# An accumulating DMA from GpSimd for the last step of most integer exponential chains, with products ordered by readiness and one set of planner limits

## The chip, the cores and the metric

The kernel runs on one core of a Trainium2 chip. The metric is the device time of one execution in microseconds. Five engines work side by side, each through its own instructions in a fixed order: PE (TensorE, matrix products), ACT (ScalarE, activations), DVE (VectorE), POOL (GpSimd) and SP (SyncE, which here issues DMAs). An engine that waits for a semaphore holds up everything that stands behind in its own order.

## The reference

The inputs are bf16. `x` has 2048 rows of 512. One branch is attention with 32 heads of 16, the other a mixer with shifted quarters of the columns and an MLP of width 1792; a sigmoid gate mixes the two. The reference, cut to what matters:

```python
def reference(A_x, A_wqkv, A_wo, B_x, B_w1, B_w2, B_w3, B_w4, gate_w):
    x = A_x                                           # 1 x 2048 x 512, bf16
    g = sigmoid((x * gate_w).sum(-1, keepdims=True))
    q, k, v = split_heads(x @ A_wqkv)                 # 32 heads of 16
    p = softmax(q @ k.T * 16 ** -0.5)                 # 2048 x 2048 per head
    a = merge_heads(p @ v) @ A_wo
    h = gelu(layernorm(x) @ B_w1)                     # 512 wide
    hs = shifted_quarters(h) @ B_w2                   # by +1, -1, +2, -2 rows
    x1 = x + hs
    b = x1 + gelu(layernorm(x1) @ B_w3) @ B_w4        # 512 -> 1792 -> 512
    return g * a + (1 - g) * b
```

## The kernel before

**Units, blocks and slots.** The attention is cut into 32 units: four chunks of 512 queries, and within each eight groups of four heads. A unit has 16 key tiles of 128 keys, and for each of them four heads, so 64 blocks of 128 keys by 512 queries. A score matmul (line 831) makes one block in PSUM. The blocks go round in slots: for each slot PE writes two or three blocks into the PSUM tile `stage`, and ACT turns them into exponentials in the SBUF ring `ring` with one activation of 1024 or 1536 columns (line 1228; in the first 34 slots into `pt`). There are two such tiles, so that PE may write the scores of slot k only when ACT is through with slot k-2. The products of the exponentials with the values (line 1241, `acc<-ring,vp`) follow in the PSUM tile `acc`. An extra column of ones in `vp` gives the denominators.

**Chains.** ACT does not take all blocks. In many slots with two blocks for ACT a third one, in the PSUM tile `dsc` beside them, goes to DVE. DVE adds a constant to the scaled score and writes an int16 (line 1048, the "dump"); these bits, read as bf16, are a piecewise linear exponential. Four blocks of one key tile are gathered in one tile of 128 x 4 x 512, 4 KB in each partition, and start a chain (the function `whole`): the exponential is smoothed by summing four copies of the bits that are shifted by `STEPS` (0, -31, -62, -95) and multiplied with weighted values (`vp` with weight 1 for the first two, `vw` with the other two weights). So a chain has three steps: each reads a term, adds an int16 constant to 128 x 2048 elements and writes another term. Steps run on DVE (line 1113) or on POOL (line 1111), whichever the planner offers them to. Each of the four terms is multiplied on PE with the values of the four heads, which makes 16 product matmuls a chain. The terms live in tiles of a pool called `room`: `quad` (three tiles), `more`, `xT` and `lent` are the names of the buffers that it is made of.

**What sets the order.** The order on every engine is planned while the program is written. A loop in Python keeps a planned time for each engine (`free`), asks for the possible next pieces of work of PE, ACT, DVE and POOL, and writes down the one that can start first. It uses fixed costs, and limits read by `rule(name)` for the unit in which the scores stand: a few usual ones (`USUAL`), and other values for many units (`RULES`). Among the limits are `CHAINS` (chains open at once), `NEED`, `AHEAD` and `HURRY` (how far ahead of a unit's end its chains start or press), `PTS` and `MANY` (how many exponentials or products may wait), `PMAX` (steps of a chain on POOL) and `BACK` (how far DVE has to be behind before POOL takes a step). The order that results is fixed in the program; the chip then runs it with semaphores. Where the plan sees PE idle for some tenths of a microsecond, the function `fill` puts a product with zeros (`acc<-wq,zero`).

`produce` puts a term's products in the list `products`, sorted by unit, in the order in which the terms are made; `attend` takes them from the front of that list. `step` makes a term from another one of the chain, `used` runs when a term's products have been placed and gives tiles back, and `opens` starts a chain after its last dump.

**Other work.** The projections, the mixer and the MLP fill PE between slots; their results leave PSUM through DVE. GELU runs on ACT between the exponentials, with a load of its table. At a unit's end DVE copies `acc` to `accsb`; SP sends the denominators through `den`, `rec_d` and the broadcast `bcs` (three DMAs, lines 1331 to 1340), and POOL multiplies (`oT<-accsb,bcs`, line 1353). POOL also does the layernorm's scaling (`xn`) and the second half of each `qT`. The limits for DVE and POOL know of a port that the two share: `post(..., shared=True)` keeps the planned time of a step on DVE away from that of one on POOL, and `behind` orders a POOL instruction after the last such step of DVE.

## Time and profile before

| what | value |
|---|---|
| median of 3 runs | 748.69 us (748.12 to 748.73) |
| the profiled execution | 748.4 us |
| its span, from the first to the last instruction | 746.6 us |
| granted TensorE clock | 1.000 |
| busy: PE, ACT, DVE, POOL | 730.8, 729.8, 683.6, 339.3 us |
| instructions: PE, ACT, DVE, POOL | 9866, 731, 1178, 295 |
| DMA: packets, bytes | 52306, 29.03 MB |

The profiled execution's own time is 1.8 us above its span, which is what lies around the first and the last instruction. "Busy" is the share of the span in which an instruction of the engine was under way; instructions overlap a little in the pipelines, and the ends of matmuls are modelled, so that a busy engine may still have small stalls inside. In a row of groups stand the line, the engine, the operation, the names written and read, their shapes and the number of instructions, then the group's busy time in us and the mean duration of one in ns, then the idle time of the engine just before them and who ended it.

### The profile page before, as it was taken

What the parts mean: (1) busy time and instruction counts of PE and PEld (TensorE: products, weight loads), DVE (VectorE), ACT (ScalarE), POOL (GpSimd) and SP (SyncE); (2) the same over time, 40 slices, a digit from 0 to 9 for tenths busy, and PEclk for the clock granted to TensorE, in tenths of its full rate; (3) what the DMA queues carried; (4) which work ended last, traced back from release to release, by engine and by line L of the source; (5) the groups of instructions that cost most, each with busy time, mean ns of one, the idle gap of its engine ahead of it and who ended that gap; (6) DMA issues with size and microseconds to landing.
All of it is one profiled execution on the core that took longest, in us unless ns stands there. A gap on an engine that the chain in (4) does not pass through costs nothing.

```text
span 746.6 us, 23400 instructions
## 1 busy us (share of the span) xinstructions
PE 730.8 (98%) x9866; PEld 230.9 (31%) x9866; DVE 683.6 (92%) x1178; ACT 729.8 (98%) x731; POOL 339.3 (45%) x295
## 2 busy tenths in 40 slices
PE   8999999999999999999999999999999999999997
PEld 4333332322332333332222332222322222322232
DVE  5799999999999998689999989999799999999994
ACT  6999999999999999999999999999999999999995
POOL 3734426444455456325564533454335455345420
PEclk9999999999999999999999999999999999999999
DMA  9400006201130060050001020000201000000011
GB/s 197 124 17 13 13 21 104 47 26 41 34 119 21 18 142 10 21 49 16 20 28 34 14 47 18 19 12 15 56 25 33 6 21 20 26 18 20 15 34 42
DMA packets 52306, 29.03 MB, mean 39 GB/s; under 512 B 36712, under 2 KB 47720, under 8 KB 52200
## 3 DMA queue, kind: packets, MB, share of 16 engines
q1 hardware_dynamic: 51240, 27.00, 15.1%
q8 instruction: 77, 1.26, 0.7%
q10 hardware_dynamic: 960, 0.52, 0.2%
q14 instruction: 29, 0.24, 0.1%
HBM read 17.17 MB, written 2.35 MB: 26 GB/s over the span
## 4 chain that ended last, share of the span: by engine, by line
PE 45%; ACT 41%; issue 10%; DVE 4%; DVEq 0%; ACTq 0%
ACT ring L1228 35%; PE acc L1241 16%; PE stage L831 14%; PE ps L301 6%; ACT pt L1228 3%; PE ps_o L301 2%; PE ps_y L301 2%; PE stage L301 1%; ACT g2T L1205 1%; DVE quad L1048 1%; ACT hT L1205 1%; ACT g2T L1208 1%; DVE xT L1048 1%; PE acc L301 1%; PE ps_q L301 1%
## 5 line engine op out<-in xcount | busy, mean ns | idle before, releaser
L1228 ACT ACTIVATE ring<-stage 128x1024 bf16<-128x1024 f32 (+1 forms) x649 | 648.3, 1159 | 1.9 <-PE dsc L831 0.5
L831 PE MATMUL stage<-qT,kT 32*128 32x512 bf16 (+2 forms) x1530 | 269.1, 380 | 6.0 <-ACT ring L1228 3.1
L831 PE MATMUL dsc<-qT,kT 16*128 16x512 bf16 (+1 forms) x542 | 208.2, 384 | 0.1
L831 PEld LDWEIGHTS <-kT 32*128 32x128 bf16 (+1 forms) x2072 | 77.0, 91 | 278.4 <-issue 250.9
L1048 DVE TENSOR_SCALAR quad<-dsc 128x512 int16<-128x512 f32 x235 | 155.1, 683 | 7.5 <-PE dsc L831 6.5
L1241 PE MATMUL acc<-ring,vp 128*17 128x512 bf16 (+3 forms) x1436 | 133.1, 378 | 1.3 <-DVE accsb L1402 0.5
L1111 POOL TENSOR_SCALAR quad<-quad 128x2048 int16<-128x2048 int16 x36 | 68.4, 1901 | 67.9 <-DVE quad L1113 22.9
L1048 DVE TENSOR_SCALAR more<-dsc 128x512 int16<-128x512 f32 x129 | 85.4, 683 | 5.5 <-PE dsc L831 4.5
L1048 DVE TENSOR_SCALAR xT<-dsc 128x512 int16<-128x512 f32 x122 | 80.5, 683 | 3.1 <-PE dsc L831 2.6
L1241 PEld LDWEIGHTS <-vp 128*17 128x17 bf16 (+1 forms) x2640 | 56.4, 89 | 81.4 <-issue 62.2
L301 PE MATMUL ps<-w,g2T 128*32 128x512 bf16 x896 | 70.2, 383 | 0.0
L1111 POOL TENSOR_SCALAR more<-more 128x2048 int16<-128x2048 int16 x20 | 38.0, 1900 | 56.8 <-DVE quad L1113 30.7
L1353 POOL TENSOR_TENSOR oT<-accsb,bcs 128x512 bf16<-128x512 f32 x29 | 37.1, 1279 | 44.6 <-DVE quad L1113 22.2
L301 PE MATMUL ps_y<-xnT,w 128*32 128x512 bf16 x704 | 54.8, 383 | 0.3 <-DVE qT L351 0.3
L1113 DVE TENSOR_SCALAR quad<-quad 128x2048 int16<-128x2048 int16 x61 | 45.6, 748 | 0.7 <-PE acc L1241 0.7
L1241 PE MATMUL acc<-quad,vp 128*17 128x512 bf16 x492 | 45.8, 381 | 0.0
L1111 POOL TENSOR_SCALAR xT<-xT 128x2048 int16<-128x2048 int16 x16 | 30.4, 1901 | 33.1 <-DVE xT L1113 7.0
L1241 PE MATMUL acc<-quad,vw 128*17 128x512 bf16 x468 | 45.2, 381 | 0.0
L1111 POOL TENSOR_SCALAR more<-quad 128x2048 int16<-128x2048 int16 x14 | 26.6, 1901 | 27.7 <-DVE quad L1113 8.1
L1048 DVE TENSOR_SCALAR lent<-dsc 128x512 int16<-128x512 f32 x56 | 37.2, 682 | 1.5 <-PE dsc L831 1.2
L1241 PEld LDWEIGHTS <-vw 128*17 128x17 bf16 x1136 | 27.8, 88 | 33.7 <-issue 25.7
L301 PEld LDWEIGHTS <-w 128*32 128x32 bf16 x1152 | 26.1, 95 | 35.3 <-issue 19.4
(146 smaller groups left out, 943.8 us busy)
## 6 DMA issues: line engine op xcount, KB each, us to landing
bcs<-rec_d SPq DMA_DIRECT2D x31, 256.0 KB
w<-in_B_w_dram SPq DMA_DIRECT2D x2, 1792.0 KB
x_sb<-in_A_x_dram SPq DMA_DIRECT2D x14, 128.0 KB
oT<-oT SPq DMA_DIRECT2D x112, 16.0 KB
out_dram<-ot SPq DMA_DIRECT2D x12, 128.0 KB
w<-in_B_w_dram SPq DMA_DIRECT2D x2, 512.0 KB
wkv<-in_A_wqkv_dram SPq DMA_DIRECT2D x1, 512.0 KB
wo_all<-in_A_wo_dram SPq DMA_DIRECT2D x8, 64.0 KB
```

What stands on the lines that cost most here:

```text
L301: nc.tensor.matmul(out[j:j + 32, :], lhsT=lhsT[:, j:j + 32], rhs=rhs, tile_position=(0, j), **kwargs)
L831: nc.tensor.matmul(out, lhsT=kT[G][32 * j:32 * j + K, cc, o:o + P], rhs=qTs[(c, G)][32 * j:32 * j + K, a, lo:hi], start=True, stop=True, t ...
L1048: nc.vector.tensor_scalar(out=bits[:, r:r + wide, :], in0=dsc.rearrange("p (a c) -> p a c", c=CH), scalar1=SHIFT, scalar2=LOWEST, op0=ALU. ...
L1111: behind(nc.gpsimd.tensor_scalar(out=to, in0=base["tile"], scalar1=1.0, scalar2=shift, op0=ALU.mult, op1=ALU.add))
L1113: fast["ins"] = nc.vector.tensor_scalar(out=to, in0=base["tile"], scalar1=shift, scalar2=None, op0=ALU.add)
L1205: nc.scalar.activation(out=part, in_=part, func=ACT.Gelu_apprx_tanh)
L1208: nc.scalar.activation(out=dst, in_=stages.pop(k)[:, 0:len(ms) * CH].rearrange("p (a c) -> p a c", c=CH), func=ACT.Gelu_apprx_tanh)
L1228: nc.scalar.activation(out=pt[:, 0:w], in_=stages.pop(k)[:, 0:w], func=ACT.Exp, scale=LN2 / 128.0)
L1241: nc.tensor.matmul(accs[n][32 * j:32 * j + M, lo:hi], lhsT=lhsT, rhs=p, start=(kt == 0), stop=(kt == NT - 1), skip_group_check=True, tile_ ...
L1353: behind(nc.gpsimd.tensor_tensor(out=oT, in0=tiles["accsb"][:], in1=tiles["bcs"][:], op=ALU.mult))
```

## The change

The last of the four terms (shift -95) is no longer made from another term by DVE or POOL in most chains. A tile of the constant -95 (`STEPS[-1] - STEPS[0]`, int16) is written once, at the start, to DRAM: POOL sets four columns of `ring`, and SP sends them to `down_d` behind the transposes of `xT`. Later, once the products of a chain's first term have been placed (`used`), POOL issues a DMA that adds `down_d` onto that first term's own tile, 128 x 2048 int16 (the function `flies`, with `accum_op=ALU.add`). Such a chain has two steps left on DVE or POOL, its steps take the newest term as their base, and its fourth term needs no further tile. A chain becomes one of this kind when fewer than `FLOWN` others (2, or 3 in units 1 to 31) have such a DMA planned or under way and it is not of the last unit. The planner's times for it are `FLIGHT`: 1.1 on POOL, 3.0 between two DMAs, 1.5 until the data have landed.

Two more things change. `produce` sorts the products of a unit by the planned time at which they are ready, where they stood in the order of their making. And `RULES` has one and the same set of limits for all units from 1 to 31, where many units had values of their own. The diff, with one line of each old and new table:

```diff
--- before.py
+++ after.py
@@ -115,6 +115,7 @@
     identf = const.tile([P, P], F32, name="identf")
     minus = const.tile([P, P], BF16, name="minus")
     rec_d = dpool.tile([NC_ * NU, 4, CH], F32, name="rec_d")
+    down_d = dpool.tile([P, 4, CH], I16, name="down_d")
 
     def wview(w):
         return w.rearrange("(kt p) c -> p kt c", p=P)
@@ -139,6 +140,9 @@
     nc.sync.dma_start(out=wkv[:, :, D:2 * D], in_=wview(A_wqkv[:, 2 * D:3 * D]))
     for c in range(1, NC_):
         nc.sync.dma_start(out=xT[c][:], in_=x_flat[c * CH:(c + 1) * CH, :], transpose=True)
+    down = ring[:, 4:8, :].bitcast(I16)
+    nc.gpsimd.memset(down, int(STEPS[-1] - STEPS[0]))
+    nc.sync.dma_start(out=down_d[:], in_=down)
     nc.gpsimd.memset(wo_pad[:], 0.0)
     nc.gpsimd.memset(pick[:], 0.0)
     for j in range(4):
@@ -167,31 +171,39 @@
 
 
 
-    USUAL = {'WIDE': 1, 'NEED': 14, 'AHEAD': 12, 'HURRY': 32, 'DLIM': 1.2, 'MANY': 8, 'PTS': 5, 'CHAINS': 2, 'MAXD': 28, 'PMAX': 3, 'BACK': 1.2, 'SHORT': 1}
+    USUAL = {'WIDE': 1, 'NEED': 14, 'AHEAD': 12, 'HURRY': 32, 'DLIM': 1.2, 'MANY': 8, 'PTS': 5, 'CHAINS': 2, 'MAXD': 28, 'PMAX': 3, 'BACK': 1.2, 'SHORT': 1, 'FLOWN': 2}
     RULES = {
-        2: {'NEED': 8, 'AHEAD': 8, 'HURRY': 14, 'DLIM': 0.9, 'MANY': 4, 'PTS': 7, 'CHAINS': 3, 'MAXD': 20, 'PMAX': 2, 'BACK': 0.9, 'SHORT': 3},
...
+        1: {'NEED': 20, 'AHEAD': 8, 'HURRY': 0, 'PTS': 6, 'PMAX': 1, 'BACK': 0.6, 'FLOWN': 3},
...
     }
     MM = 0.214
     TURN = 0.104
@@ -222,6 +234,7 @@
     DFILL = 1
     SLACK = 0.25
     GAP = 0.3
+    FLIGHT = (1.1, 3.0, 1.5)
     AGE = 4.0
     ARANK = 3
     LAG = 2.0
@@ -233,7 +246,7 @@
     free = {"pe": NOWFREE, "act": NOWFREE, "vector": NOWFREE, "pool": NOWFREE}
     queue = {"pe": [], "act": [], "vector": [], "pool": []}
     state = {"n": 0, "gen": 0, "young": True, "mm": 0, "sp": 0.0, "before": True, "after": False, "aside": 0.0, "kind": "", "t": 0.0, "piece": 0.0,
-             "credit": 0.0, "mixable": 0, "done": False, "ending": False, "acc": 0.0, "raw": 0, "moved": False, "accsb": 0.0, "slot": 0, "outs": 0, "bank": 0}
+             "credit": 0.0, "mixable": 0, "done": False, "ending": False, "acc": 0.0, "raw": 0, "moved": False, "accsb": 0.0, "slot": 0, "outs": 0, "bank": 0, "flown": 0.0}
     asides = deque()
     at = {}
     banks = {0: 0.0, 1: 0.0, 2: 0.0}
@@ -260,6 +273,7 @@
         return sum(min(b, t) - max(a, t - WINDOW) for a, b in busy if b > t - WINDOW) / WINDOW
 
     fast = {"ins": None}
+    flown = []
 
     def behind(ins):
 
@@ -1017,7 +1031,7 @@
 
     def produce(n, *term):
         i = len(products)
-        while i and products[i - 1][0] > n:
+        while i and (products[i - 1][0], products[i - 1][4]) > (n, term[3]):
             i -= 1
         products.insert(i, (n, *term))
 
@@ -1053,7 +1067,7 @@
             if full:
                 post("vector", rank(), 0.69, opens, begins(end), True)
 
-        terms, chain = [], {"next": 1, "pool": 0, "held": 2, "left": 0, "offers": []}
+        terms, chain = [], {"next": 1, "pool": 0, "held": 2, "left": 0, "offers": [], "flown": False}
 
         def give(tile, t):
             freed[id(tile)] = t
@@ -1066,6 +1080,8 @@
         def used(term):
             def go(t):
                 term["free"] = max(t, term["read"])
+                if chain["flown"] and not term["i"]:
+                    return post("pool", -1, FLIGHT[0], lambda end: flies(term["tile"], end), term["free"])
                 spare = [x for x in terms if x["free"] is not None and not x["gone"]]
                 if len(spare) > chain["left"]:
                     spare[0]["gone"] = True
@@ -1076,6 +1092,14 @@
             term = {"tile": tile, "i": i, "free": None, "gone": False, "read": 0.0}
             terms.append(term)
             produce(n, kt, heads, tile, end + HOLD[other], i == len(STEPS) - 1, used(term), i)
+
+        def flies(tile, end):
+            behind(nc.gpsimd.dma_start(out=tile, in_=down_d[:], accum_op=ALU.add))
+            state["flown"] = max(state["flown"], end) + FLIGHT[1]
+            lands = state["flown"] + FLIGHT[2]
+            flown.remove(None)
+            flown.append(lands)
+            produce(n, kt, heads, tile, lands, True, lambda t: give(tile, t), len(STEPS) - 1)
 
         def ready_tile(end):
             def go():
@@ -1091,7 +1115,7 @@
             i = chain["next"]
             chain["next"] += 1
             done = [x for x in terms if x["free"] is not None and not x["gone"] and x["free"] <= end - cost]
-            base = next(x for x in terms if not x["gone"])
+            base = terms[-1] if chain["flown"] else next(x for x in terms if not x["gone"])
             if chain["held"]:
                 chain["held"] -= 1
                 chain["times"].pop(0)
@@ -1119,7 +1143,7 @@
                         x["gone"] = True
                         give(x["tile"], x["free"])
             chain["pool"] += other
-            if chain["left"] == 1:
+            if chain["left"] == 1 - chain["flown"]:
                 quad["chains"] -= 1
 
         def opens(end):
@@ -1129,6 +1153,12 @@
             chain["tiles"] = [room.popleft(), room.popleft()]
             chain["times"] = [freed.get(id(x), 0.0) for x in chain["tiles"]]
             add(bits, 0, end - 0.69)
+            while flown and min(x or 1e9 for x in flown) < end:
+                flown.remove(min(x or 1e9 for x in flown))
+            if len(flown) < rule("FLOWN") and n < len(units) - 1:
+                chain["flown"] = terms[0]["gone"] = True
+                chain["left"] -= 1
+                flown.append(None)
             one(end, False, 0.69)
             offer("pool", 1.9, end)
 
```

The whole program is planned anew, so that nearly every row moves. Counted in the two orders: the steps of chains are 303 on DVE and 123 on POOL before, 242 and 50 in the change; POOL has 134 DMAs onto terms that were not there. The number of chains is 142 in both (2272 products of terms, 16 a chain). ACT has 535 activations of 1024 columns and 114 of 1536 into `ring` before, 532 and 116 in the change; together with the 34 into `pt` that is 1480 blocks in both. The products with zeros are 328 matmuls before and 408 in the change, four of which run side by side.

The first place is POOL in the middle of the program, where its steps stand between the multiplications `oT`. Before (`quad`, `more` and `xT` are tiles of `room`; behind each row the semaphores that it waits for, where PE, DVE or Pool is an engine and DMAHW a DMA issued by SP):

```order
L1353 TENSOR_TENSOR oT<-accsb,bcs 128x512 [waits DMAHW4_49,DMAHW3_49,DMAHW5_49,DMAHW2_49,DMAHW0_49]
L1353 TENSOR_TENSOR oT<-accsb,bcs 128x512 [waits DMAHW3_49,DMAHW2_49,DMAHW4_49,DMAHW1_49,DMAHW7_49,DVE_49,Pool_49]
L1111 TENSOR_SCALAR more<-more 128x2048 [waits DVE_49,PE_49] x2
L1111 TENSOR_SCALAR quad_273<-quad_273 128x2048 [waits DVE_49,PE_49]
L1111 TENSOR_SCALAR more<-quad_272 128x2048 [waits DVE_49,PE_49]
L1111 TENSOR_SCALAR xT_113<-quad_272 128x2048 [waits PE_49]
L1111 TENSOR_SCALAR more<-quad_274 128x2048 [waits DVE_49,PE_49]
L1111 TENSOR_SCALAR quad_273<-quad_273 128x2048 [waits DVE_49,PE_49]
L1111 TENSOR_SCALAR quad_273<-quad_272 128x2048 [waits DVE_49,PE_49,Pool_49]
L1353 TENSOR_TENSOR oT<-accsb,bcs 128x512 [waits DMAHW6_49,DMAHW5_49,DMAHW7_49,DMAHW4_49,DMAHW2_49]
```

In the change, at such a place (DMASW is a DMA issued by POOL):

```order
L1097 DMA xT_114<-down_d 128x2048 [waits DMASW0_49,DVE_49,PE_49]
L1135 TENSOR_SCALAR xT_113<-more 128x2048 [waits DVE_49,PE_49]
L1097 DMA quad_277<-down_d 128x2048 [waits PE_49]
L1097 DMA more<-down_d 128x2048 [waits DMASW6_49,DVE_49,PE_49]
L1097 DMA quad_275<-down_d 128x2048 [waits PE_49]
L1097 DMA quad_276<-down_d 128x2048 [waits DMASW4_49,DVE_49,PE_49]
L1135 TENSOR_SCALAR more<-xT_114 128x2048 [waits DMASW2_49,DVE_49,PE_49]
L1383 TENSOR_TENSOR oT<-accsb,bcs 128x512 [waits DMAHW5_49,DMAHW4_49,DMAHW6_49,DMAHW3_49,Pool_49]
L371 TENSOR_SCALAR qT<-qT,second 128x512 [waits DVE_49]
L1097 DMA more<-down_d 128x2048 [waits DMASW5_49,DVE_49,PE_49]
```

Between two `oT` there were seven steps in this piece; now there are DMAs and one step. Each DMA waits for PE, which has to be through with the first term's products, and everything behind it on POOL waits as well.

The second place is PE, where it reads a term that another engine has made. Before, for a term that POOL wrote (`stage` and `dsc` are the scores of one slot, `vw_162` the weighted values):

```order
L831 MATMUL stage<-qT,kT_141 128x512 [waits Activation_49]
L831 LDWEIGHTS kT_141
L831 MATMUL stage<-qT,kT_141 128x512
L831 LDWEIGHTS kT_141
L831 MATMUL dsc<-qT,kT_141 128x512 [waits DVE_49]
L1241 LDWEIGHTS vw_162
L1241 MATMUL acc<-more,vw_162 17x512 [waits Pool_49]
```

In the change, for the term that the row `DMA quad_277<-down_d` of the piece above makes. First the end of the products of that tile's first use, as first term, with the unweighted values `vp_157`; the DMA waits for these:

```order
L1271 MATMUL acc<-quad_277,vp_157 17x512
L1271 LDWEIGHTS vp_157
L1271 MATMUL acc<-quad_277,vp_157 17x512
L1271 LDWEIGHTS vp_157
L1271 MATMUL acc<-more,vp_157 17x512
L1271 LDWEIGHTS vp_157
```

Then, with the scores of six slots in between, the place where PE reads the same tile again as fourth term, with the weighted values `vw_163`:

```order
L845 MATMUL dsc<-qT,kT_138 128x512 [waits DVE_49]
L1271 LDWEIGHTS vw_161
L1271 MATMUL acc<-xT_113,vw_161 17x512
L1271 LDWEIGHTS vw_161
L1271 MATMUL acc<-xT_113,vw_161 17x512
L1271 LDWEIGHTS vw_161
L1271 MATMUL acc<-xT_113,vw_161 17x512
L1271 LDWEIGHTS vw_161
L1271 MATMUL acc<-xT_113,vw_161 17x512
L1271 LDWEIGHTS vw_163
L1271 MATMUL acc<-quad_277,vw_163 17x512 [waits DMASW1_49]
```

The wait for Pool has become a wait for a DMA that POOL issues, and the time that this DMA has is the time that PE takes from the one place to the other. Counted in the order in the same way, of the 133 DMAs that wait for PE 33 have six slots or fewer in between (nine of them five or fewer), 31 have seven, and 69 have eight to fourteen.

52 lines of the change are left out of this document (30 added, 22 removed).

## The prediction

> **What bounds the kernel now.** I read the page first: the span, the busy times and the chain that ended last.
>
> ```profile
> span 746.6 us, 23400 instructions
> PE 730.8 (98%) x9866; PEld 230.9 (31%) x9866; DVE 683.6 (92%) x1178; ACT 729.8 (98%) x731; POOL 339.3 (45%) x295
> PE 45%; ACT 41%; issue 10%; DVE 4%; DVEq 0%; ACTq 0%
> ```
>
> PE and ACT are both at 98% and share the chain between them; DVE, which the change relieves, has 4% of it. Next come the groups of ACT, first from the page, then by shape.
>
> ```profile
> L1228 ACT ACTIVATE ring<-stage 128x1024 bf16<-128x1024 f32 (+1 forms) x649 | 648.3, 1159 | 1.9 <-PE dsc L831 0.5
> ...
> L1228 ACT ACTIVATE ring<-stage 128x1024 bf16<-128x1024 f32 x535 | 505.0, 1082 | 1.5 <-PE dsc L831 0.5
> L1228 ACT ACTIVATE ring<-stage 128x1536 bf16<-128x1536 f32 x114 | 163.0, 1517 | 0.5 <-PE stage L831 0.3
> L1228 ACT ACTIVATE pt<-stage 128x1024 bf16<-128x1024 f32 x34 | 31.4, 1091 | 0.6 <-PE stage L831 0.5
> ```
>
> The exponentials take 648.3 + 31.4 = 679.7 us, with 2.6 us of visible idle time. Whether small waits are hidden inside, the timeline of ACT tells where it runs without any: the start of a tight run, and the start of one further on in the same run.
>
> ```profile
> 17.56 11.10 ACT L1228 ACTIVATE pt<-stage 128x1024 bf16<-128x1024 f32 x12
> 27.50 1.16 ACT L1228 ACTIVATE pt<-stage 128x1024 bf16<-128x1024 f32 x1
> 732.15 5.48 ACT L1228 ACTIVATE ring<-stage 128x1536 bf16<-128x1536 f32 x4
> 733.48 1.46 ACT L1228 ACTIVATE ring<-stage 128x1536 bf16<-128x1536 f32 x1
> ```
>
> Eleven activations of 1024 columns later is 9.94 us later, 0.904 us each; one of 1536 takes 1.33 us. So 569 x 0.904 + 114 x 1.33 = 666.0 us is what the exponentials cost when PE is always in time. They take 679.7 + 2.6 = 682.3, so about 16.3 us of the span are scores that come late. This is all that a better order can win as long as ACT keeps its blocks.
>
> Who makes the scores late? The waits of PE's weight loads and of PE (us in total, times, the longest):
>
> ```profile
> PEld L831 <- issue: 250.9, 648, 0.7
> ...
> PEld L831 <- DVE quad L1048: 7.3, 18, 0.6
> PEld L831 <- DVE xT L1048: 4.2, 10, 0.4
> PEld L831 <- DVE quad L1113: 3.8, 9, 0.4
> PEld L831 <- DVE more L1113: 3.0, 7, 0.4
> PEld L831 <- DVE more L1048: 2.1, 5, 0.4
> ...
> PEld L831 <- DVE lent L1048: 1.3, 3, 0.4
> ...
> PE stage L831 <- ACT ring L1228: 3.1, 11, 0.5
> ```
>
> A load for scores that waits for nobody has 250.9 / 648 = 0.39 us of idle time before it. The 52 that DVE released have 21.7 us, 0.42 each, so DVE added only 21.7 - 52 x 0.39 = 1.4 us. Most of the 16.3 us are not DVE's: PE is late because it is just at something else in its order.
>
> **The change part by part.** *ACT's work.* By the order there are 3 activations of 1024 fewer and 2 of 1536 more: -3 x 0.904 + 2 x 1.33 = -0.05 us, nothing. The number of chains is the same, 142, so no block leaves ACT.
>
> *Steps taken off DVE and POOL.* All steps of DVE, then all of POOL:
>
> ```profile
> 0.00:746.70 746.70, 207.89 (x303) 1.00 0.16 39
> ...
> 0.00:746.70 746.70, 233.74 (x123) 1.00 0.16 39
> ```
>
> A step is 207.89 / 303 = 0.686 us on DVE and 233.74 / 123 = 1.90 us on POOL. DVE loses 61 steps, 41.8 us, and falls to some 642 us; POOL loses 73, 138.7 us. None of this is on the path by itself. What it can win is lateness: at least 0, at most the 16.3 us. I take the 1.4 us that DVE visibly added, and of the other 14.9 us a share of 0.17, a little under the 61/303 = 0.20 by which DVE's steps become fewer, since the evictions that scores wait for most (line 1048) stay as they are: 1.4 + 2.6 = 4.0 us. Low and high end are 0 and -16.3.
>
> *134 issues on POOL.* No DMA is issued by POOL before. The nearest rows are SP's issue of a broadcast and POOL's own pass over such a tile (1.90 us):
>
> ```profile
> L1340 SPq DMA_DIRECT2D bcs<-rec_d x31: 562/577/594, 45.5 to 725.9; - x31
> ```
>
> Between 0.58 and 1.90 us I take 1.1, the planner's own figure in the diff: 134 x 1.1 = 147 us, so that POOL stays about as busy as it was (339.3 - 138.7 + 147 = 348 of 747). Covered: POOL is free half of the time. But POOL works in order, and a DMA that waits for PE's products holds up the next DMA, the steps, `xn` and `oT` behind it; `oT` in turn holds up DMAs while `bcs` has not landed.
>
> *The flight.* It has two bounds in the trace. A load of weights moves at 332 to 355 GB/s, and the 256 KB of one `bcs`, issued at 45.46, are through before 50.4:
>
> ```profile
> 211.60:213.60 2.00, 1.90 (x35) 0.81 (x29) 1.97 (x4) 2.00 (x3) 0.00 (x0) 1.00 1.03 332
> 264.20:266.20 2.00, 1.93 (x30) 0.70 (x26) 1.95 (x5) 2.00 (x3) 1.90 (x2) 1.00 1.03 355
> ...
> 45.46 0.58 SPq L1340 DMA_DIRECT2D bcs<-rec_d  x1
> ...
> 46.40:47.40 1.00, 1.00 (x26) 0.49 (x27) 1.00 (x2) 1.00 (x2) 0.82 (x2) 1.00 0.14 39
> 48.40:49.40 1.00, 1.00 (x23) 0.47 (x20) 1.00 (x3) 1.00 (x2) 0.00 (x0) 1.00 0.26 100
> 49.40:50.40 1.00, 1.00 (x19) 0.26 (x11) 1.00 (x3) 1.00 (x3) 0.00 (x0) 1.00 0.05 18
> 50.40:51.40 1.00, 1.00 (x17) 0.26 (x9) 1.00 (x4) 1.00 (x3) 0.00 (x0) 1.00 0.00 0
> ```
>
> A term has 524,288 bytes, 1.5 us at the pace of the load and 3.0 if adding in place moves them twice; at the pace of `bcs` (about 3 us for half as much) it is 6. Ahead of that stand some 1.4 us from the issue of `bcs` to its first bytes (45.46 to about 46.8, by the rise in the rows). So from PE's last product on the first term to the use of the fourth it is at least 1.5 + 1.4 = 2.9 us and at most 6 + 1.4 = 7.4. I take 6.0, because the plan spaces for 1.1 + 3.0 + 1.5 = 5.6, whose middle term is the doubled load, and 0.39 us is the nearest row for a hand-over to PE. By *DMA: Bandwidth & Descriptors*, section "Anatomy of one DMA — SWDGE (gpsimd) path", in the Trainium skill, such a DMA takes 2.0 us plus its bytes at 436 GB/s, here an estimate of 3.2 us, or 4.4 with the bytes twice; by that no term would be late and the sum would be that of the first rival, 744.4. No run here shows it.
>
> What is there for it: ACT's work on slots begins at 9.07 and its last four activations, in the row above, end at 732.15 + 5.48 = 737.63.
>
> ```profile
> 9.07 31.50 ACT L1228 ACTIVATE pt<-stage 128x1024 bf16<-128x1024 f32 x34 [0.50 <-PE stage L831]
> ```
>
> With 14 of GELU there are 697 slots in these 728.6 us, 1.05 us a slot. Six slots are 6.3 us, seven 7.3. By the order 33 of 133 flights have six slots or fewer, so a flight of 6.0 is just in time. What makes it late is company. The 31 `bcs` move 3 us each, and a flight moves 3.0; with 134 flights in 690 us, one in 5.15, each `bcs` meets (3 + 3) / 5.15 = 1.17 of them, 36 in all, and delays them by half its time, 1.5 us. A quarter of these (33/133), 9, are of the tight ones, late by 6.0 + 1.5 - 6.3 = 1.2 us. ACT has a cushion: while PE waits one activation still runs, 0.904 us, less the 0.384 of a score matmul:
>
> ```profile
> L831 PE MATMUL stage<-qT,kT x1530: 214/384/386, 8.6 to 735.3; 16*128 16x512 bf16 x94, 32*128 32x512 bf16 x93, 32*128 32x128 bf16 x3, 32*128 32x256 bf16 x2
> ```
>
> That is 0.52 us. So 9 x (1.2 - 0.52) = 6.1 us. With the short flight this term is 0, with the long one some 20 to 45.
>
> *The rest.* `bcs` itself may be delayed by a flight; before, the engines of its readers sat idle for it three times in all:
>
> ```profile
>   DMA bcs<-rec_d: 7.9, 3
> ```
>
> Nothing taken, up to 2 us if it reaches PE through `accsb`. The constant's write at the start stands on SP's queue ahead of twelve loads of `x_sb` and takes at most 1.5 us of the DMA engines; nothing taken. The 80 further zero matmuls are 20 groups of 0.22 us and stand where the plan sees PE idle: nothing taken, 4.4 at most. The new limits and the sorting of products change which piece of PE's work stands ahead of which slot; before, this made most of the 16.3 us, and I see no reason for a sign.
>
> The sum against the profiled execution: 748.4 - 4.0 + 6.1 = 750.5. The median of the runs is 0.3 above it, so 750.8.
>
> **The rivals.** *All terms in time.* If a flight is under 6.3 + 0.52 - 1.5 = 5.3 us, even a delayed one costs nothing, and 748.4 - 4.0 = 744.4 is left, 744.7 against the median. For it speaks the pace of the weight loads; against it that adding in place has to read what it writes.
>
> *Nothing reaches ACT.* DVE's relief was never on the path (1.4 us seen), and the terms are in time or the two cancel: 748 to 750. The change then doesn't do what it is named for.
>
> *Long flights.* From 6.8 us on, also flights without company are late. At 7.4, 33 x (7.4 - 6.3 - 0.52) = 19 us and more for those with company: 765 to 785. For it speaks the pace of `bcs`.
>
> *The port.* POOL's steps often begin when one of DVE has ended:
>
> ```profile
> L1111 POOL TENSOR_SCALAR quad<-quad 128x2048 int16<-128x2048 int16 x36 | 68.4, 1901 | 67.9 <-DVE quad L1113 22.9 <-DVE xT L1113 15.9 <-DVE more L1113 12.0
> ```
>
> The plan keeps the two apart. If a step of DVE that comes while POOL issues delays the DMA by its 0.69 us, the nine late ones lose 9 x 0.69 = 6.2 us more: 757. *SBUF — State Buffer*, "Who interferes with whom", in the Trainium skill says that a step of DVE that uses both its ports shuts GpSimd out while it writes the descriptors of a DMA; the trace agrees only in that the two alternate.
>
> **How the numbers follow.** A few terms late, 750.8: 0.34. All in time, 744.7: 0.32. Nothing reaches ACT, 749: 0.19. The port, 757: 0.06. Long flights, 765 and up: 0.09. The first, fourth and fifth are slower, 0.49 in all, the second is faster; the bound for a difference is 0.2%, 1.5 us, about what this kernel's measurement can tell. The forecast is that of the first. It stands only just above that bound, and its own range is 750.2 to 757, from one delayed term less than counted to twice as many. Over all, 743 leaves out 0.08 of the second case, where more than a third of the hidden lateness goes, and 764 the fifth.
>
> **What would show it.** In the profile after, ACT's exponentials and their idle time should again sum to some 682 us, DVE's steps to 166 us, POOL's to 95. PE's waits for DMAs issued by POOL should be some ten, of about a microsecond. If they are none, the flight is shorter than 5.3 us and the second rival holds; if over thirty, it is longer than 6.8. The forecast is wrong in its sign if the new order brings the scores in time for reasons of PE's own work, which I could not price.

## The result: 870.5 us, 16% slower, and the profile after

The median of four runs of the change is 870.54 us (865.02 to 883.16), that of the kernel before beside it 748.71. The ratio is 1.160, with a 95% interval of 1.154 to 1.167; the longest run, 883.16, is not in it. The forecast of 750.8 and the range up to 764 were wrong by far. The profiled execution took 873.04 us. A flight is, as in the prediction, one of the 134 DMAs that POOL issues onto a first term; a flown term is what it leaves in the tile. From the page:

```profile
span 871.2 us, 23744 instructions
...
PE 806.9 (93%) x9946; PEld 232.4 (27%) x9946; DVE 661.7 (76%) x1113; ACT 745.4 (86%) x730; POOL 327.4 (38%) x357
...
PEclk9996998867779898999999999879699888999779
DMA  9364549777946496566576775548755566667621
...
q0 software_dynamic: 19296, 70.26, 47.0%
q1 hardware_dynamic: 51384, 27.53, 15.0%
...
PE 52%; DMA 22%; ACT 9%; DVE 6%; issue 6%; SPq 4%; POOL 1%; DVEq 0%; POOLq 0%; ACTq 0%
...
L1258 ACT ACTIVATE ring<-stage 128x1024 bf16<-128x1024 f32 (+1 forms) x648 | 663.4, 1121 | 110.1 <-PE dsc L845 91.4
```

ACT's share of the chain fell from 41% to 9%, and DMAs, which had none, have 22%. ACT now sits idle for 110.1 us before its exponentials, where it was 1.9. PE tells more. It is busy for 806.9 us instead of 730.8, with nearly the same products (9946 against 9866), and idle for 871.2 - 806.9 = 64.3 us instead of 15.8. The two differences, 76.1 and 48.5, make up the whole 124.6 us by which the span grew.

The busy part grew because the granted clock is no longer 9 in every slice: its mean is 0.900. It has two values here, full and half, so that PE was at half clock for 2 x (1 - 0.900) x 871.2 = 174 us. The idle part is in the waits of PE, then POOL and SP (us in total, times, the longest):

```profile
PE acc L1271 <- DMA quad<-down_d: 18.1, 11, 3.2
PE acc L1271 <- DMA lent<-down_d: 13.4, 7, 2.8
PE acc L1271 <- DMA more<-down_d: 10.4, 9, 2.5
PE acc L1271 <- DMA xT<-down_d: 3.4, 5, 1.3
...
POOL oT L1383 <- DMA bcs<-rec_d: 74.5, 18, 8.4
...
SPq L1370 <- DMA rec_d<-rec: 109.0, 31, 7.1
```

PE waits 32 times for a flown term, 45.3 us. POOL waits 18 times for a broadcast `bcs`, 74.5 us; before, all readers of `bcs` together waited three times, 7.9 us. SP waits for `rec_d`, a transfer of 8 KB, before it may issue the broadcast: 109.0 / 31 = 3.5 us each. Before it was 1.3:

```profile
SPq L1340 <- DMA rec_d<-rec: 41.5, 31, 3.0
```

So small transfers that have nothing to do with the flights take over twice as long. DVE's own work is not slowed: a dump of one block takes 685 ns, before 683. The flights themselves, from the line that issues them (duration of the issue on POOL in ns, then the time to landing):

```profile
L1097 POOL DMA_DIRECT2D quad<-down_d x57: 834/887/1523, 47.2 to 833.6; - x57
...
DMA to landing us min/median/max: 5.2/6.0/12.1
```

The windows around the first long wait show how wait and clock hang together (length, busy time of PE, PEld, DVE, ACT and POOL with instructions, granted clock, share of the DMA engines, GB/s):

```profile
57.00:60.40 3.40, 3.40 (x65) 1.45 (x61) 2.67 (x8) 3.40 (x5) 0.84 (x1) 1.00 0.85 180
60.40:61.40 1.00, 1.00 (x23) 0.39 (x16) 0.78 (x2) 1.00 (x3) 0.00 (x0) 1.00 0.98 148
...
61.80:65.20 3.40, 1.01 (x19) 0.41 (x18) 0.67 (x4) 0.88 (x2) 1.26 (x1) 1.00 0.85 166
65.20:68.60 3.40, 3.40 (x37) 0.60 (x25) 2.85 (x6) 2.87 (x3) 1.89 (x1) 0.50 0.13 30
68.60:72.00 3.40, 3.40 (x29) 0.73 (x26) 1.89 (x3) 2.05 (x2) 0.89 (x1) 0.50 0.02 2
...
78.90:82.30 3.40, 3.40 (x34) 0.81 (x31) 2.24 (x5) 1.99 (x3) 0.00 (x0) 0.50 0.58 111
82.30:85.70 3.40, 3.40 (x60) 1.25 (x60) 2.92 (x7) 3.25 (x4) 1.32 (x2) 1.00 0.30 51
```

And the timeline of PE at that place (start, length in us, in brackets the idle time ahead):

```profile
64.19 0.39 PE L1271 MATMUL acc<-lent,vw 128*17 128x512 bf16 x4 [2.76 <-DMA lent<-down_d]
...
66.58 0.60 PE L845 MATMUL stage<-qT,kT 16*128 16x512 bf16 x2
```

Up to 61.40 PE is busy all the time. Then it waits 2.76 us for `lent`, which has not landed, and in the 3.40 us to 65.20 it is busy for 1.01. From 65.20 on the clock is 0.50, for five windows; a matmul takes 0.60 us instead of 0.39, and PE gets through 29 to 37 of them in a window instead of 60 to 65. The wait of 2.8 us has cost more than itself.

By the clock's records there are 17 such stretches, all on one grid of 3.41 us, one to seven steps long. Cutting the trace by that grid, the window ahead of each stretch had PE busy for 0.21 to 0.63 of it; of 187 windows that were followed by full clock all but the very first had 0.61 or more. The Trainium skill, *TensorE: Matmul & The Clock Gate*, "Part 1: The HAM clock gate (the "warmup" mystery)", gives the window (3413 ns, free-running) and says that half clock follows an idle window and ends after one busy window or more. The trace agrees on the length. It differs on the first condition: no wait here is longer than 3.2 us, so a window that is half busy is enough. On the second it shows that one busy window need not do: the stretch above lasts through five in which PE is busy throughout.

### The profile page after: what moved, and what is told of

Read it like the earlier page. It is cut to its first block, busy times and chain, and to the rows that moved or that the text cites. A ratio compares the mean times of both kernels' runs of the same rounds, so it can differ in the third digit from the quotient of the medians.

```text
span 871.2 us, 23744 instructions
## 1 busy us (share of the span) xinstructions
PE 806.9 (93%) x9946; PEld 232.4 (27%) x9946; DVE 661.7 (76%) x1113; ACT 745.4 (86%) x730; POOL 327.4 (38%) x357
## 4 chain that ended last, share of the span: by engine, by line
PE 52%; DMA 22%; ACT 9%; DVE 6%; issue 6%; SPq 4%; POOL 1%; DVEq 0%; POOLq 0%; ACTq 0%
PE acc L1271 18%; PE stage L845 16%; ACT ring L1258 8%; DMA more<-down_d 6%; DMA quad<-down_d 5%; PE ps L315 5%; DMA lent<-down_d 4%; SPq L465 3%; PE ps_y L315 3%; DMA xT<-down_d 3%; DMA bcs<-rec_d 2%; PE stage L315 2%; DMA rec_d<-rec 2%; PE acc L315 2%; PE ps_v L315 2%
## 5 line engine op out<-in xcount | busy, mean ns | idle before, releaser
L1258 ACT ACTIVATE ring<-stage 128x1024 bf16<-128x1024 f32 (+1 forms) x648 | 663.4, 1121 | 110.1 <-PE dsc L845 91.4
L845 PE MATMUL stage<-qT,kT 16*128 16x512 bf16 (+2 forms) x1533 | 289.8, 410 | 3.4 <-DVE quad L1062 1.5
L845 PE MATMUL dsc<-qT,kT 32*128 32x512 bf16 (+1 forms) x539 | 224.8, 418 | 0.0
L845 PEld LDWEIGHTS <-kT 16*128 16x128 bf16 (+1 forms) x2072 | 72.5, 92 | 315.2 <-issue 286.6
L1097 POOL DMA_DIRECT2D quad<-down_d x57 | 56.4, 1004 | 111.4 <-PE acc L1271 54.9
L1383 POOL TENSOR_TENSOR oT<-accsb,bcs 128x512 bf16<-128x512 f32 x29 | 37.2, 1282 | 86.0 <-DMA bcs<-rec_d 74.5
L1097 POOL DMA_DIRECT2D more<-down_d x36 | 33.7, 942 | 75.2 <-PE acc L1271 52.1
L1097 POOL DMA_DIRECT2D xT<-down_d x26 | 26.1, 1016 | 64.9 <-PE acc L1271 24.4
L315 PE MATMUL acc<-wq,zero 128*32 128x512 bf16 x408 | 41.7, 451 | 0.0
L1271 PE MATMUL acc<-more,vw 128*17 128x512 bf16 x284 | 31.4, 434 | 10.6 <-DMA more<-down_d 10.4
L1353 DVE COPY accsb<-acc 128x512 f32<-128x512 f32 x31 | 21.3, 687 | 24.1 <-PE acc L1271 16.0
```

The lines of the kernel that those rows point to most:

```text
L315: nc.tensor.matmul(out[j:j + 32, :], lhsT=lhsT[:, j:j + 32], rhs=rhs, tile_position=(0, j), **kwargs)
L845: nc.tensor.matmul(out, lhsT=kT[G][32 * j:32 * j + K, cc, o:o + P], rhs=qTs[(c, G)][32 * j:32 * j + K, a, lo:hi], start=True, stop=True, t ...
L1097: behind(nc.gpsimd.dma_start(out=tile, in_=down_d[:], accum_op=ALU.add))
L1258: nc.scalar.activation(out=pt[:, 0:w], in_=stages.pop(k)[:, 0:w], func=ACT.Exp, scale=LN2 / 128.0)
L1271: nc.tensor.matmul(accs[n][32 * j:32 * j + M, lo:hi], lhsT=lhsT, rhs=p, start=(kt == 0), stop=(kt == NT - 1), skip_group_check=True, tile_ ...
L1353: nc.vector.tensor_copy(out=accsb[:], in_=acc[:])
```

## The experiments

Theory A: terms land late, PE waits, and the clock falls after the longer waits. B: the new order, with its limits and the sorting, is bad by itself. C: the flights' traffic delays the other transfers. For every kernel the profiled execution gives PE's busy and idle time (span less busy) and the time at half clock, 2 x (1 - mean clock) x span; the last column is SP's wait for `rec_d` in us. The first row is the kernel before as measured beside the experiments.

| kernel | median us | PE busy | PE idle | half clock | rec_d |
|---|---|---|---|---|---|
| before | 748.5 | 730.8 | 15.8 | 0 | 41.5 |
| the change | 870.5 | 806.9 | 64.3 | 174 | 109.0 |
| 1 no flight | 762.0 | 738.8 | 22.4 | 14 | 42.1 |
| 2 unread | 814.9 | 753.0 | 57.5 | 57 | 111.9 |
| 3 quarter | 754.9 | 733.3 | 17.8 | 3 | 54.5 |
| 4 guard | 843.6 | 790.8 | 51.6 | 72 | 112.5 |
| 5 small packets | 888.5 | 796.4 | 90.2 | 154 | 96.4 |
| 6 copy | 773.8 | 736.8 | 29.2 | 18 | 75.8 |
| 7 later | 859.5 | 796.5 | 63.1 | 110 | 102.3 |
| 8 sorted | 770.8 | 750.7 | 18.7 | 8 | 35.7 |
| 9 long waits | 862.9 | 771.9 | 68.4 | 97 | 36.8 |
| 10 short waits | 804.0 | 754.8 | 51.8 | 58 | 35.3 |
| 11 no waits | 749.3 | 731.9 | 15.5 | 0 | 36.2 |
| 12 one flight | 806.7 | 765.4 | 37.3 | 64 | 59.4 |

**1, no flights.**

```diff
-            if len(flown) < rule("FLOWN") and n < len(units) - 1:
+            if len(flown) < 0 and n < len(units) - 1:
```

> The change with no flown terms: every chain makes its fourth term by a step again; the one set of limits and the sorting of products stay. Theory A, late terms (PE waits for terms that land late, and the granted clock falls after the longer waits): no such wait is left and the clock stays at 1.00. By the order ACT has 541 activations of 1024 columns and 142 of 1536, by the rows of before 541 x 0.904 + 142 x 1.33 = 677.9 us against 666.0, so 748.7 + 12 = 761, between 750 and 775. Theory B, the order (the limits and the sorting are bad by themselves): 830 or more, with the same kind of waits on PE for DVE and POOL. Theory C, DMA traffic (the flights delay bcs and with it POOL and accsb): as A, 761.

Measured 762.0 (ratio 1.019, 1.014 to 1.023). B is out as the main cause: limits and sorting without flights cost about what theory A allows for the work that ACT gets from seven chains fewer, 12 us. One thing missed: the clock did not stay at 1.00. There is one stretch of 14 us at half clock, and no long wait of PE ahead of it; the window before it had PE busy for 0.75.

**2, the flown term is not read.**

```diff
-            produce(n, kt, heads, tile, lands, True, ...)
+            produce(n, kt, heads, None, lands, True, ...)   # None: wq[:, 0, :] is read
```

> The change in the same order, but the products of a flown term read a tile of constants (the query weights) in place of the flown tile; the DMAs all stay. Left out: the fourth term's share of the result. Theory A: PE waits for no DMA of POOL, the clock stays at 1.00, and the time falls to 750 to 765. Theory B: nothing changes, some 870. Theory C: the broadcasts bcs stay slow, POOL's oT still wait some 75 us for them, DVE's accsb waits stay, and the time stays over 800.

Measured 814.9 (1.088, 1.083 to 1.093). That is over 800, as theory C has it, and POOL's waits for `bcs` stay; but 55.6 us of the loss are gone, which is A's part, so both hold. PE waits for no flight any more, but for others:

```profile
POOL oT L1383 <- DMA bcs<-rec_d: 79.4, 18, 8.9
PE ps_y L315 <- DMA xnT<-xn: 11.6, 2, 8.4
PE acc L1271 <- DVE accsb L1353: 7.2, 5, 2.2
PE ps_y L315 <- DMA oT<-oT: 6.7, 1, 6.7
PE stage L315 <- DMA xnT<-xn: 6.0, 1, 6.0
```

The mixer's transposes (`xnT`) and the attention's outputs (`oT`) come late, single waits of 6 to 8 us; before, no transfer made PE wait.

**3, a quarter of the bytes.**

```diff
-            behind(nc.gpsimd.dma_start(out=tile, in_=down_d[:], accum_op=ALU.add))
+            behind(nc.gpsimd.dma_start(out=tile[:, 0:1, :], in_=down_d[:, 0:1, :], accum_op=ALU.add))
```

> The change in the same order, but each DMA adds onto the first quarter of its tile only, 128 KB. Left out: three quarters of the fourth term's last shift. Theory A, with a flight whose length is set by its bytes: issue to landing falls from a median of 6.0 us to some 3 to 4, PE's waits for it from 32 (45 us) to under 8, and the time falls to 750 to 770. If the flight is long for a reason that doesn't go by bytes (issue, adding in place), it stays over 5 us and the time over 850. Theory B: some 870 either way. Theory C: oT's waits for bcs fall from 74.5 us to under 25, together with A, so that only the unread run tells C from A.

Measured 754.9 (1.008, 1.006 to 1.010). The order and the number of issues on POOL are those of the change, and nearly the whole loss is gone. The flights' queue on its page, their landing, and the waits:

```profile
q0 software_dynamic: 19296, 17.57, 16.7%
```

```profile
DMA to landing us min/median/max: 3.1/3.6/8.8
```

```profile
PE acc L1271 <- DMA quad<-down_d: 4.8, 2, 3.3
...
POOL oT L1383 <- DMA bcs<-rec_d: 7.5, 2, 5.7
```

Landing takes 3.6 us instead of 6.0, PE waits twice for a flight, and `bcs` is as early as before.

So POOL's issues, the rearranged steps and the order together cost 6 us, and the bytes cost 115: 60 of them without the terms being read (run 2 against 3), nearly all through other transfers, and 55.6 more when the terms are read (the change against run 2). Not all of the 60: in run 2 DVE and POOL also wait 8.7 us for a flight to land before they use its tile again.

The two parts aren't two sets of waits laid end to end. In the profiled executions the change idles only 6.8 us more than run 2 (64.3 against 57.5), but it is busy for 53.9 us more, with 117 us more at half clock. Its 45.3 us of waits for flights stand where run 2 waits for something else: PE's waits for `xnT` and `oT`, 24.3 us in run 2, are 1.9 in the change. What reading the terms costs is mostly the clock.

**4, zero products ahead of the late terms.**

```diff
+                    for _ in range(COVER.get(state["guard"], 0)):   # 7 for 12 flights, 4 for 9
+                        strips(accs[n][:], lhsT=zero[:], rhs=wq[:, 0, :], start=False, stop=False, ...)
```

> The change, with zero products of 0.22 us ahead of the 21 flown terms for which PE waited longest: seven ahead of 12 (waits of 1.9 us or more), four ahead of 9 (0.8 to 1.7 us), 26 us of such work in all, which stands where PE waits anyhow. Theory A with the falling clock as the larger part (76 of the 124 us): the stretches at half clock fall from 17 (174 us) to eight or fewer, and the time falls by 40 to 75 us, to 800 to 830. Rival: the clock falls for a reason other than PE's idle time, or the half clock costs nothing by itself: 17 stretches or so remain, and the time stays at 865 to 900.

Measured 843.6 (1.125, 1.121 to 1.129). Half clock fell from 174 to 72 us in eight stretches, as theory A has it, but the time fell by only 27, not by 40 or more. PE still waits 34 us for flights: 11.6 us behind the zero products and 22.5 at terms that have none ahead, so that much of the 26 us of zero products was added work. By the 0.40 us for each us at half clock that runs 9 and 10 give, below, 102 us less of half clock are 41 us less of busy time; with 26 more that is 15, and PE's busy time fell by 16.1.

**5, packets of 1 KB.**

```diff
-    down_d = dpool.tile([P, 4, CH], I16, name="down_d")
+    down_d = dpool.tile([P, 4, CH + 32], I16, name="down_d")   # written and read as down_d[:, :, 0:CH]
```

> The change in the same order with the same bytes, but the constant lies in DRAM with 64 spare bytes after each 1024, so that a flight should go as 512 packets of 1 KB instead of 128 of 4 KB. Theory D, other transfers wait behind one long packet on each DMA engine (a packet of 4 KB takes 0.38 us in the change, one of 1 KB 0.11 in the quarter run): SP's wait for rec_d falls from 109 us to some 41.5 + (109 - 41.5) / 4 = 58, oT's wait for bcs to under 25, and the time to 780 to 815, the flights themselves being as long as before. Theory E, the flights take the engines' time whatever the packet (3 us for 512 KB): the waits stay at 100 to 115 us and the time at 860 to 880. Third case: POOL pays for the number of packets when it issues; then an issue takes 2 us or more instead of 0.89, and the time goes over 900.

Measured 888.5 (1.185, 1.179 to 1.190), a little above the range of theory E and far from D. SP waits little less for `rec_d`, 96.4 us, though `oT`'s waits for `bcs` halved, 37.9 us. PE's waits for flights rose from 45.3 to 79.4 us. The flights grew longer, and so did their issue:

```profile
q0 software_dynamic: 70752, 70.26, 54.8%
```

```profile
L1097 POOL DMA_DIRECT2D quad<-down_d x57: 1180/1233/2117, 46.8 to 850.9; - x57
...
DMA to landing us min/median/max: 5.6/7.1/13.9
```

The packets are nearly four times as many, the issue takes 1.23 us, and landing 7.1. So it isn't mainly the length of one packet by which a flight holds up the others, and shorter packets only make it slower.

**6, a copy in place of an addition.**

```diff
-    nc.gpsimd.memset(down, int(STEPS[-1] - STEPS[0]))
+    nc.gpsimd.memset(down, 16000)
-            behind(nc.gpsimd.dma_start(out=tile, in_=down_d[:], accum_op=ALU.add))
+            behind(nc.gpsimd.dma_start(out=tile, in_=down_d[:]))
```

> The change in the same order with the same bytes, but the DMA overwrites the tile with a constant (16000) in place of adding. Left out: the fourth term itself. Theory F, adding in place is what makes a packet long: a packet of 4 KB falls from 0.38 us to about the 0.16 us of the constant's own write, a flight by 8 packets x 0.22 = 1.8 us to some 4.2, SP's wait for rec_d from 109 us to 55 to 70, and the time to 755 to 775. Rival: the source in DRAM or the writing of the tile limits the packet; it stays over 0.3 us and the time over 840.

Measured 773.8 (1.037, 1.032 to 1.041), in the range of theory F; SP's wait for `rec_d`, 75.8 us, is a little above it.

```profile
q0 software_dynamic: 19296, 70.26, 28.4%
```

```profile
DMA to landing us min/median/max: 3.4/4.1/15.7
```

A flight takes 0.284 x 766.0 / 134 = 1.62 us of all 16 engines, against 0.470 x 871.2 / 134 = 3.06 with the addition. Adding in place nearly doubles it. With the same bytes, this run loses 25 us and the change 122, so what the flights cost goes by the time that they take of the engines and not by their bytes alone.

**7, a longer flight in the plan.**

```diff
-    FLIGHT = (1.1, 3.0, 1.5)
+    FLIGHT = (1.0, 3.6, 5.5)
```

> The change with the planner's times for a flight at 1.0, 3.6 and 5.5 us in place of 1.1, 3.0 and 1.5: by the order 101 flights with six slots at least and a median of 13. ACT takes more blocks itself: 536 x 0.904 + 152 x 1.33 = 686.7 us against 666.0, 20.8 more. If late landing were the whole loss, 748.5 + 21 = 770. With the loss shared as the first four runs have it (60 us from the quarter run to the unread one, which is traffic, and 55 more from there to the change, which is late terms), PE's waits for flights are gone (under 5 us), the traffic stays, 101/134 x 60 = 45 us, and the time is 748.5 + 21 + 45 = 815, between 795 and 830.

Measured 859.5 (1.146, 1.141 to 1.151), 45 us above the expectation. PE's waits for flights are gone, 2.5 us, yet it idles for 63.1. Of the chain's long pieces (start, length) one is a flight and most others are small transfers, among them:

```profile
153.39 10.55 DMA den<-accsb
...
316.09 7.38 DMA oT<-oT
...
443.01 7.96 DMA rec_d<-rec
...
543.76 14.69 DMA xT<-down_d
```

What the expectation had not counted are the zero products that the plan puts in, 924 matmuls against 408, by their groups 81.9 us against 35.5 in run 3. Those alone are as much as the 45 us, but 110 us at half clock lengthen PE's work too, so the split is open. Planning the flight at about its length does not save the change.

**8, sorted products alone, on the kernel before.**

```diff
-        while i and products[i - 1][0] > n:
+        while i and (products[i - 1][0], products[i - 1][4]) > (n, term[3]):
```

> The kernel before with one part of the change: products sorted by readiness; no flights and the limits of before. By the order ACT has 573 activations of 1024 and 110 of 1536, 664.3 us against 666.0, and 143 chains. If the sorting is harmless, 747 us, between 745 and 750. If it is what makes the change slow, 755 or more.

Measured 770.8 (1.029, 1.028 to 1.031): with the old limits the sorting alone costs 22 us. That is the second case by its number, but not the cause it named: sorting and the change's limits together do no such harm (runs 1 and 3). No run has those limits without the sorting. PE is 19.9 us busier, and zero products are 18.9 of it (first before, then sorted):

```profile
L301 PE MATMUL acc<-wq,zero 128*32 128x512 bf16 x308 | 26.8, 383 | 0.0
```

```profile
L301 PE MATMUL acc<-wq,zero 128*32 128x512 bf16 x520 | 45.7, 383 | 0.0
```

**9 to 11, waits put into the kernel before.** No part of the change is in these.

```diff
+        if hold["due"] is None and k >= hold["k"] and accs and k < 670:
+            probe()                                                  # zero product that reads held
+            nc.sync.dma_start(out=held[0:16, :], in_=x_flat[0:16, 0:P])
+            hold["k"], hold["due"] = hold["k"] + 30, k + D           # D = 0, 1, 6
+        if hold["due"] is not None and k >= hold["due"] and accs:
+            probe()
```

> The kernel before with 21 waits put into PE, one every 30 slots: a zero product that reads a small tile, a DMA of 4 KB from SP onto that tile, and directly behind it a second zero product that reads it. PE idles from the one to the other, some 2.3 us by SP's issue (0.58) and the 1.34 us that a small DMA takes in the trace of before. Theory G, the clock goes by windows of 3.41 us, and one with PE busy for less than some 0.62 of it is followed by half clock: a wait of 2.3 us falls over 1.26 us into one window nine times in ten, so 15 to 21 stretches at half clock, of 3.4 to 10 us each, and each us of them costs PE 0.43 us (in the change 76 us of 174): 21 x 2.3 = 48 us of idle time and 25 to 85 us of slow products, time 820 to 880. Rival, the waits cost only themselves: no or few stretches, time 785 to 797.

> The same 21 pairs, but with one slot (1.05 us) between the DMA and the second product, so that PE idles some 1.2 us each time. Theory G: under the 1.26 us that a window allows, so few stretches at half clock (0 to 5); 21 x 1.2 = 25 us of idle time, part of it taken up by the cushion of ACT, time 765 to 785. Rival, every wait costs in proportion, clock and all: half of what the long waits add.

> The same 21 pairs with six slots between the DMA and the second product: the same work and DMAs, and nobody waits. Both theories: no stretch at half clock, 748 to 755.

The waits of the three, in the order 9, 10, 11:

```profile
PE acc L303 <- DMA held<-in_A_x_dram: 55.0, 21, 7.0
```

```profile
PE acc L303 <- DMA held<-in_A_x_dram: 37.8, 21, 7.1
```

```profile
PE acc L303 <- DMA held<-in_A_x_dram: 0.9, 1, 0.9
```

The same 21 pairs cost nothing to speak of without a wait (749.3), 55 us with waits of 1.8 us on average (804.0) and 114 with 2.6 (862.9). The profiled executions took 749.2, 808.4 and 842.0 us; in them half clock is 0, 58 and 97 us in 0, 6 and 12 stretches, and PE is busier than in run 11 by 22.9 and 40.0 us: 0.39 and 0.41 us for each us at half clock. That settles the amplification without any flight: by the same 0.40, 174 us are 70 of the change's 76.1 us. Twelve stretches are fewer than the 15 to 21 expected, though the time is in its range. The short waits were longer than expected (1.8, not 1.2) and so missed 765 to 785, and with that the bound of 1.26 us was not tested: in the profiled executions each us of PE's waits costs 1.6 us of time in run 10 and 1.7 in run 9, which the rival, cost in proportion, says as well. Nor is the bound on the busy share sharp. In run 9 eight windows with PE busy for 0.61 or less were followed by full clock, and in runs 1, 2, 5 and 8 five stretches followed windows with 0.64 to 0.75.

**12, one flight at a time.**

```diff
-        1: {..., 'FLOWN': 3},
+        1: {..., 'FLOWN': 1},      # and in USUAL
```

> The change with at most one flight planned or under way at a time (FLOWN is 1 everywhere): 61 flights instead of 134. By the order ACT has 543 activations of 1024 columns, 139 of 1536 and one of 512: 675.7 us against 666.0, so 10 us more. If the loss goes with the number of flights, 61/134 of the 115 us that lie between the quarter run and the change: 748.5 + 10 + 52 = 811. If it comes of several flights behind one another (a second or third lands late and holds up the small transfers for 6 us and more), it falls by more than the number: 760 to 775, SP's wait for rec_d under 65 us and PE's waits for flights under 8.

Measured 806.7 (1.078, 1.074 to 1.082), by the number of flights. The traffic is light here, as the second case said (`rec_d` 59.4, `oT` waits for `bcs` once, 2.4 us), but the terms are late all the same:

```profile
PE acc L1271 <- DMA more<-down_d: 7.8, 5, 2.4
PE acc L1271 <- DMA quad<-down_d: 7.8, 6, 3.5
PE acc L1271 <- DMA lent<-down_d: 4.4, 3, 2.0
```

```profile
DMA to landing us min/median/max: 5.2/5.6/8.8
```

Those 21 us of waits, and 64 us at half clock, which are 26 us by the 0.40, are 47 of the 58 us that this kernel loses. So late terms cost most of it with little traffic beside them; the rest is as much as the 10 us of ACT's extra blocks. None of these kernels beats the one before.

## Why the prediction was wrong, step by step

Three terms failed: *the flight*, taken at 6.0 us and measured at 7.3; *the rest*, where the delay of other transfers stood at nothing and cost most of 60 us; and the clock, which had no term and brought some 70 us, inside what the other two cost.

*ACT's work unchanged* was right: the exponentials have the same shapes, and run 3, with all of the new order, ends at 754.9.

*The relief of DVE and POOL, -4.0 us*, had the right work and the wrong effect. The steps became 168.09 us on DVE and 94.66 on POOL, as announced (166 and 95), but no lateness went with them. In run 3 the exponentials and their idle time are 648.6 + 7.3 and 31.4 + 0.6, 687.9 us, against 682.3 before; ACT's idle time of 1.2 and 2.8 us right behind PE's two waits for flights is most of the difference. In the change itself, where the prediction named a sum of some 682 us as a sign, it is 663.4 + 110.1 + 31.4 + 0.6 = 805.5.

```profile
L1258 ACT ACTIVATE ring<-stage 128x1024 bf16<-128x1024 f32 (+1 forms) x648 | 648.6, 1152 | 7.3 <-PE dsc L845 6.0 <-PE acc L1271 0.5 <-ACT ring L1258 0.2
L1258 ACT ACTIVATE pt<-stage 128x1024 bf16<-128x1024 f32 x34 | 31.4, 1093 | 0.6 <-PE stage L845 0.5
```

*The issue, 1.1 us*, is 0.89 in the median and 0.99 on average. It is covered, as taken: run 3 has all 134 and loses 6 us.

*The flight, 6.0 us from PE's last product to use* is the term that failed first. Issue to landing alone has a median of 6.0 and a minimum of 5.2. Ahead of it, by the trace's times of products and issues, POOL issues some 0.5 us after PE's last product in the median, and up to about 5. (The trace names tiles without the buffer's number, so these are as near as the names tell.) From that product to the last byte it is in the median 7.3 us, and 8.5 or more for a quarter of the flights. So "Long flights", which I gave 0.09, held as a mechanism, with its sign of over thirty waits; but the upper bound of 7.4 was only the median, and 765 to 785 for it still 85 us too low. The price of the wait was wrong too: 32 waits of 1.4 us on average, where nine of 0.7 were counted. The fit that the Trainium skill gives in *DMA: Bandwidth & Descriptors*, section "Anatomy of one DMA — SWDGE (gpsimd) path", an estimate of 3.2 us for such a DMA, is not borne out: the trace has a median of 6.0, and the copy of run 6 has 4.1, at least 3.4.

*Company* was counted on the wrong side. I let 36 flights be delayed by a `bcs`. What was delayed were the transfers beside the flights, and those set down as nothing: `bcs`, 74.5 us of POOL's waits instead of 7.5, and with it the DMAs that stand behind `oT` on POOL; `den`, `rec_d`, `xnT` and `oT`. I had the engines' time right (3.0 us a flight, measured 3.06), and did not ask what a load that rises from 15% to 62% of the engines does to chains of three transfers in a row. That is most of the 60 us between runs 3 and 2.

*The cushion.* That ACT's 0.52 us absorb the first part of a wait holds only where PE can catch up. PE had 15.8 us of idle time in all. Against run 11, the waits of run 10 are 36.9 us longer and PE's idle time is 36.3 us longer, so next to nothing is caught up.

*The clock* had no term at all. The granted clock before stood at 1.000, and I took it for a constant; runs 9 to 11 show that it answers to PE's idle time. By their 0.40 us for each us, some 70 of the 124.6 us came by it. Run 3, which has the same products in the same order, bears that out: PE is busy there for 733.3 us with 3 at half clock, 73.6 less than in the change.

*The zero products* stood at nothing, 4.4 at most. In run 3 they are 35.5 us against 28.8 before, 6.7 more, and with the 22 us for the sorting under the old limits this shows a place where a changed order is paid for.

*The port*, a rival, can't be large: run 3 has all issues and steps in their order and loses 6 us altogether.

## What to carry to other kernels

Where PE has no idle time to spare, a wait of PE for a transfer is paid more than once (1.6 us and more for each us in runs 9 and 10), since a window that is half idle can bring half clock for the next ones. So compare the slack that an order leaves a DMA with its landing under load, and not with its bytes alone. Repairs that cost PE work win little of it back: zero products through the waits won 27 us here, a longer flight in the plan 11. Before moving arithmetic into DMAs, add up what share of the DMA engines it will take, and list the small transfers in chains that will share them; here the arithmetic was cheap on DVE, and 70 MB of additions in place were not cheap beside 28 MB of others. Test the bytes and the order apart: the same order with a quarter of each transfer showed that it cost 6 of the 122 us.

## What the runs showed of the chip that I had not expected

- In the change, half clock follows a 3.41 us window in which PE was busy for 0.63 or less, although it was never idle for a whole one. A stretch lasts one to seven windows (eight once, in run 9), also while PE is busy throughout, and each us of it costs this kernel 0.40 us. Why some stretches last so long stays open, and so does why five in other runs followed windows that were busier.
- A DMA of 512 KB that adds in place takes 3.06 us of all 16 engines, a copy of the same bytes 1.62, and the same addition in 1 KB packets 0.548 x 886.6 / 134 = 3.63. POOL is held for 0.89 us by the issue of the first and for 1.23 by that of the last.
- With the DMA engines at 62%, SP's wait for an 8 KB transfer is 3.5 us on average instead of 1.3. In run 7, at 51%, a single `den` took 10.6 us and a `rec_d` 8.0.
